# The second wq slice loaded through GpSimd's queue, x tiles 0 to 3 in order on SyncE's

## The chip, the cores and the metric

The kernel runs on one core of a Trainium2 chip. A core has five engines that run side by side, each with its own list of instructions: TensorE (PE in the profile; its weight loads are PEld), VectorE (DVE), ScalarE (ACT), GpSimd (POOL) and SyncE (SP), which here only issues transfers. SyncE, ScalarE and GpSimd each have a queue of their own for transfers; the transfers themselves run on the core's 16 DMA engines. Engines wait for one another through semaphores.

The metric is the time of one execution on the device in microseconds (us), the median of several runs.

## The reference

Two blocks work on the same x of 2048 tokens by 640 features (bfloat16), and a gate mixes them:

```
q, k, v = split(x @ wqkv)              # 32 heads of 20
phi(t)  = (t + 1 if t > 0 else exp(t)) + 1e-6
a = (phi(q) @ (phi(k)^T v)) / (phi(q) . sum(phi(k)) + 1e-6) @ wo      # per head
h = gelu(layernorm(x) @ w1), its four column quarters shifted by 1, -1, 2, -2 tokens, @ w2
x1 = x + h ;  b = x1 + gelu(layernorm(x1) @ w3) @ w4
out = g * a + (1 - g) * b,   g = sigmoid(x . gate_w)
```

Only the first lines matter here: the change lies in the first microseconds, in which the q of the first 512 tokens is made.

## The kernel before

Tokens are cut into 16 tiles of 128, features into five slices of 128 (KD = 5). The weights of q, wq, are five slices of 128 rows by 640 columns, one load of 160 KB each; an x tile is one load of the same size. A product of q for one tile needs x transposed, so for tiles 0 to 3 TensorE transposes the five 128 by 128 blocks of a tile into PSUM (`t_x`, matmuls of line 617) and VectorE copies them to `xT` (line 671). From tile 4 on the transposing is done by transfers (line 285).

`q_four` makes q for tiles 0 to 3. It hands to `stream` a list of steps, which TensorE runs in exactly this order: (t, None) is the transposing of tile t, (t, k) adds the product of tile t with slice k to the tile's accumulator, by one matmul of 512 columns (line 889) and one of 128 (line 890). When a tile has had its fifth slice, `phi` evacuates it: an exponential on ScalarE (line 662), a minimum and an addition (line 628) and the last combination (line 645) on VectorE. An accumulator takes two of the eight PSUM banks, and a bank is given out again when its evacuation is done. The list is written so that a step stands about where its tile or slice is expected.

Behind `q_four` come the k products of tile 0 (`k_first`, line 910) and then of tiles 1 to 3 (line 606), and from there on q and k tile by tile; then the sums over tokens on TensorE and VectorE, the two layernorm blocks and the output. All of these are items that a planner (`_Items.run`) strings together: it takes at each step the item that can start first by a model of costs (`_Sched.simulate`), which also gives out the PSUM banks. Within `q_four` nothing is planned.

The loads of the start are issued in program order on their queues. Before the change ScalarE's queue has slice 0 of wq, and SyncE's has x tiles 0, 1 and 3, slice 1, x tile 2, slices 2, 3 and 4, the five slices of wk, the gate weights, and x tiles 4 to 7 in one load (lines 690 to 699, through the helpers at lines 679 to 686; the issuing instruction is always line 289, the gate weights' line 288). GpSimd begins with a memset of two columns of wkg (line 688), and then makes constants (lines 725 to 739): the identity for the transposes, masks, zeros. Its own queue is used later, for w1, w2, wv and wo.

Of the kernel before, what the change touches and what calls it, by code (L numbers as in the profile page):

```python
# [416 lines left out]
def _build(nc, A_x, A_wqkv, A_wo, B_w1, B_w2, B_w3, B_w4, gate_w, out, dbg=None, stop=None):  # L417
# [246 lines left out]
    def memset(engf, ap, val):  # L664
        return engf(lambda e: e.memset(ap, val), [], [ap])
# [19 lines left out]
    def load_wq(k, queue="sp"):  # L685
        sch.dma(queue, wq[:, k, :], A_wqkv[128 * k:128 * (k + 1), 0:D], "wq%d" % k)

    memset(pool, wkg[:, :, D:D + 2], 1.0)
    load_wq(0, "act")
    for load, i in ((load_x, 0), (load_x, 1), (load_x, 3), (load_wq, 1), (load_x, 2), (load_wq, 2), (load_wq, 3), (load_wq, 4)):  # L690
        load(i)
    for k in range(KD):
        dma_in(wkg[:, k, 0:D], A_wqkv[128 * k:128 * (k + 1), D:2 * D], "wk%d" % k)
# [67 lines left out]
    def phi(b, dst, after_exp=None):  # L761
        n = nfree(dst)
        er = Er[:, slot("E", 3), 0:n]
        src = psf[:, 512 * b:512 * b + n]
        activation(er, src, ACTF.Exp)
        if after_exp is not None:
            after_exp()
        ts(dve, er, er, 1.0, EPS_PHI, ALU.min, ALU.add)
        return stt(dst, src, 1.0 + EPS_PHI, er, ALU.add, ALU.max)
# [103 lines left out]
    def stream(order, w, n2, done):  # L873
        bs = {}
        for t, k in order:
            if k is None:
                if t is None:
                    warmup(WARM2, 0.42)
                else:
                    t_x(t)  # L880
                continue
            if k == 0:
                bs[t] = pair()
                bank_hold.update((bs[t], bs[t] + 1))
            b = bs[t]
            l = xT[:, k, 128 * t:128 * (t + 1)]

            def fn(e, l=l, b=b, k=k):
                e.matmul(ps[:, b, 0:512], l, w[:, k, 0:512], start=(k == 0), stop=(k == KD - 1))  # L889
                return e.matmul(ps[:, b + 1, 0:n2], l, w[:, k, 512:512 + n2], start=(k == 0), stop=(k == KD - 1))  # L890
            pe(fn, [w[:, k, 0:512 + n2], l], [ps[:, b, 0:512], ps[:, b + 1, 0:n2]], cost=272.0)
            if k == KD - 1:
                bank_hold.difference_update((b, b + 1))
                done(t, b)

    def q_four():
        order = [(1, None), (0, 0), (3, None), (1, 0), (0, 1), (1, 1), (3, 0), (3, 1), (2, None), (0, 2), (1, 2), (0, 3), (0, 4), (1, 3),
                 (1, 4), (3, 2), (3, 3), (3, 4), (2, 0), (2, 1), (2, 2), (2, 3), (2, 4)]
        stream(order, wq, 128, lambda t, b: phi(b, pq_tok[:, t + 1, :]))

    def k_out(t, b):
# [16 lines left out]
    addA(("tx", 0), 0.28, lambda: t_x(0, (0, 1, KD)))  # L918
    addA(("warm", 1), 0.0, lambda: warmup(WARM2, 0.42))
    addA(("q", 3), 5.44, q_four)  # L920
    addA(("k", 0), 1.36, k_first)
    for i in range(1, 4):
# [399 lines left out]
    for t in range(NT):  # L1322
        deps = [(("zb",), 1.0), (("qr", max(t // 4, 1)), 2.0)]
        if t < 7:
            i = (5 * t) // 2 + 3
# [3 lines left out]
        else:  # L1329
            i = 3 * (t - 7)  # L1330
# [41 lines left out]
    order = IT.run(sch, hook)  # L1372
# [6 lines left out]
def bass_gated_mix__linear_attn_block__mixer_s_mlp__prompt_kernel(  # L1379
    nc, A_x, A_wqkv, A_wo, B_x, B_w1, B_w2, B_w3, B_w4, gate_w, out  # L1380
):
    assert tuple(A_x.shape) == (1, S, D) and tuple(out.shape) == (1, S, D)
    assert tuple(A_wqkv.shape) == (D, 3 * D) and tuple(A_wo.shape) == (D, D)
    assert tuple(B_w1.shape) == (D, D) and tuple(B_w2.shape) == (D, D)
    assert tuple(B_w3.shape) == (D, F) and tuple(B_w4.shape) == (F, D) and tuple(gate_w.shape) == (D,)
    _build(nc, A_x, A_wqkv, A_wo, B_w1, B_w2, B_w3, B_w4, gate_w, out)
# [28 lines left out]
```

## Time and profile before

| what | value |
|---|---|
| median of three runs | 260.2 us (259.57 to 260.27) |
| profiled execution | 260.19 us |
| its span (first to last instruction) | 258.4 us |
| TensorE busy | 252.7 us, 98% of the span |
| granted TensorE clock | 1.0 |
| VectorE, ScalarE, GpSimd busy | 158.5, 110.9, 97.0 us |

The span is shorter than the execution, since launching and finishing lie around it. Times in the profile are counted from the start of the span. A busy TensorE need not be TensorE at its peak. A transfer has two times: that of its issue, which holds the issuing engine, and that of its landing, for which others wait. "Idle before" is the time for which an engine stood still ahead of an instruction, with what ended it. A wait for several semaphores is put down to the one that came last.

The order on SyncE's queue before, by start in us: x tile 0 at 0.79, x tile 1 at 1.25, x tile 3 at 1.71, slice 1 of wq at 2.18, x tile 2 at 2.66, slices 2 to 4 from 3.13, the wk slices from 4.55, the gate weights at 6.93, x tiles 4 to 7 at 7.40.

### The profile page before, as it was taken

The page shows a single profiled execution, that of the slowest core. Times are in us where ns is not written, and L with a number is a line of the kernel's source. Part 1 is how long each engine was busy: PE and PEld are TensorE (multiplying, and loading weights), DVE is VectorE, ACT ScalarE, POOL GpSimd, SP SyncE. Part 2 cuts the span into 40 slices and gives each one's busy share as a digit, 9 for nine tenths or more (in the row PEclk, how much of TensorE's full clock was granted, in tenths as well). Part 3 has the DMA queues.
Part 4 walks back from the last instruction along what each step waited for, and adds up shares of the span by engine and source line. Part 5 has one row for each costly group of instructions (what it writes and reads, how often), then busy time and mean ns, then how long its engine had stood idle before and what let it go on. Part 6 is the DMA issues. An engine that isn't in the chain of part 4 may idle for free.

```text
span 258.4 us, 3797 instructions
## 1 busy us (share of the span) xinstructions
PE 252.7 (98%) x1400; PEld 122.0 (47%) x1427; DVE 158.5 (61%) x293; ACT 110.9 (43%) x229; POOL 97.0 (38%) x154
## 2 busy tenths in 40 slices
PE   7999999999999999999999999999999999999996
PEld 2555555544445455555444444444444444444443
DVE  2597877899954699989995302999022530134076
ACT  1496777741355856694864240005500045200100
POOL 8004996869944119659681210111020120021000
PEclk9999999999999999999999999999999999999999
DMA  6858997826528699483667512114200140000324
GB/s 193 264 94 239 140 138 196 231 56 122 102 46 108 115 382 322 85 100 65 127 123 118 101 20 23 25 25 129 43 3 0 20 124 0 0 0 1 43 84 139
DMA packets 58644, 26.78 MB, mean 104 GB/s; under 512 B 49966, under 2 KB 57215, under 8 KB 58626
## 3 DMA queue, kind: packets, MB, share of 16 engines
q1 hardware_dynamic: 57122, 22.92, 42.6%
q0 software_dynamic: 1168, 3.28, 5.5%
q10 hardware_dynamic: 336, 0.35, 0.4%
q8 instruction: 11, 0.18, 0.3%
q14 instruction: 7, 0.06, 0.1%
HBM read 12.09 MB, written 2.67 MB: 57 GB/s over the span
## 4 chain that ended last, share of the span: by engine, by line
PE 80%; DVE 12%; DMA 3%; ACT 2%; issue 1%; SPq 1%; DVEq 0%
PE ps L606 53%; PE ps L1229 22%; DVE qprod L636 7%; DMA wq<-in_A_wqkv_dram 2%; DVE x_tok L643 2%; PE ps L889 1%; ACT h2T L662 1%; PE ps L788 1%; DMA xnT<-xn 1%; PE ps L1116 1%; DVE pq_tok L1143 1%; PE ps L1204 1%; DVE dnr L1126 1%; ACT junk L661 1%; DVE zsum L636 1%
## 5 line engine op out<-in xcount | busy, mean ns | idle before, releaser
L606 PE MATMUL ps<-xnT,w 128*128 128x512 bf16 x351 | 80.0, 379 | 0.6 <-DMA xnT<-xn 0.2
L606 PEld LDWEIGHTS ps<-xnT,w 128*128 128x128 bf16 x360 | 34.6, 98 | 39.3
L645 DVE SCALAR_TENSOR_TENSOR x_tok<-ps,stg,abx 128x512 bf16<-128x512 f32 (+2 forms) x17 | 12.2, 717 | 58.2 <-PE ps L1229 48.4
L1229 PE MATMUL ps<-w,h2T 128*128 128x512 bf16 (+2 forms) x215 | 46.4, 366 | 0.3
L628 POOL TENSOR_SCALAR abx<-x_tok,stg 128x512 f32<-128x512 bf16 x16 | 12.1, 756 | 88.1 <-DVE x_tok L645 70.0
L628 POOL TENSOR_SCALAR xn<-x_tok,st 128x640 bf16<-128x640 bf16 x32 | 38.6, 1219 | 8.8 <-DMA xnT<-xn 8.4
L662 ACT ACTIVATE h2T<-ps 128x512 bf16<-128x512 f32 x52 | 29.8, 599 | 22.8 <-PE ps L606 22.8
L1229 PEld LDWEIGHTS ps<-w,h2T 128*128 128x128 bf16 x221 | 21.1, 98 | 24.1
L662 ACT ACTIVATE tlT<-ps 128x512 bf16<-128x512 f32 x8 | 4.8, 597 | 64.1 <-PE ps L606 41.9
L662 ACT ACTIVATE Er<-ps 128x640 bf16<-128x640 f32 (+1 forms) x35 | 23.0, 659 | 17.8 <-PE ps L606 9.6
L661 ACT ACTIVATE junk<-x_tok 128x640 bf16<-128x640 bf16 x32 | 23.6, 737 | 4.7 <-DVE x_tok L643 4.2
L662 ACT ACTIVATE hsT<-ps 128x512 bf16<-128x512 f32 (+1 forms) x32 | 18.9, 594 | 14.2 <-PE ps L606 13.8
L606 PE MATMUL ps<-w,hsT 128*128 128x128 bf16 (+1 forms) x159 | 23.8, 298 | 0.1
L606 PE MATMUL ps<-wkg,xT 128*128 128x512 bf16 (+1 forms) x148 | 22.5, 298 | 0.2
L606 PE MATMUL ps<-M_sb,pqnT 128*128 128x512 bf16 x78 | 19.3, 379 | 0.2
L606 PEld LDWEIGHTS ps<-w,hsT 128*128 128x128 bf16 x160 | 13.4, 98 | 12.5
L645 DVE SCALAR_TENSOR_TENSOR abx<-ps,stg,abx 128x512 f32<-128x512 f32 x16 | 12.0, 749 | 10.7 <-PE ps L606 7.2
L606 PEld LDWEIGHTS ps<-wkg,xT 128*128 128x128 bf16 x150 | 12.6, 97 | 11.7
L808 PE MATMUL ps<-pk_tok,x_tok 128*128 128x512 bf16 x78 | 17.7, 379 | 0.1
L643 DVE SCALAR_TENSOR_TENSOR x_tok<-ps,x_tok 128x640 bf16<-128x640 f32 x16 | 13.1, 821 | 7.5 <-PE ps L606 6.9
L636 DVE TENSOR_TENSOR qprod<-qprod,pk_tok 128x640 f32<-128x640 f32 x13 | 16.3, 1253 | 0.5
L628 DVE TENSOR_SCALAR Er<-Er 128x640 bf16<-128x640 bf16 (+1 forms) x35 | 11.6, 332 | 7.6 <-ACT Er L662 6.8
(85 smaller groups left out, 280.7 us busy)
## 6 DMA issues: line engine op xcount, KB each, us to landing
w<-in_B_w_dram SPq DMA_DIRECT2D x1, 2160.0 KB, 9.7
w<-in_B_w_dram SPq DMA_DIRECT2D x1, 2080.0 KB, 15.4
x_tok<-in_A_x_dram SPq DMA_DIRECT2D x3, 640.0 KB, 5.7
out_dram<-x_tok SPq DMA_DIRECT2D x3, 640.0 KB, 3.5
w<-in_B_w_dram POOLq DMA_DIRECT2D x8, 160.0 KB, 5.9
wkg<-in_A_wqkv_dram SPq DMA_DIRECT2D x5, 160.0 KB, 4.1
wv<-in_A_wqkv_dram POOLq DMA_DIRECT2D x1, 800.0 KB, 5.7
x_tok<-in_A_x_dram SPq DMA_DIRECT2D x4, 160.0 KB, 3.3
```

Source lines behind the costliest of these rows:

```text
L606: ins = e.matmul(out_ap, l, r, start=(i == 0), stop=(i == n - 1))
L628: return engf(lambda e: e.tensor_scalar(out_ap, in_ap, s1, s2, op0, op1), rd, [out_ap], cost=cost)
L636: return engf(lambda e: e.tensor_tensor(out_ap, a, b_, op), [a, b_], [out_ap], cost=cost)
L643: return dve(lambda e: e.scalar_tensor_tensor(out_ap, in0, scalar, in1, op0, op1, accum_out=accum), rd, [out_ap, accum], cost=cost + 70.0)
L645: return dve(lambda e: e.scalar_tensor_tensor(out_ap, in0, scalar, in1, op0, op1), rd, [out_ap], cost=cost)
L661: return act(lambda e: e.activation(out_ap, in_ap, func, bias=bias, scale=scale, accum_out=accum), rd, wr, cost=cost)
L662: return act(lambda e: e.activation(out_ap, in_ap, func, bias=bias, scale=scale), rd, wr, cost=cost)
L788: e.matmul(ps[:, b, :], l, x_tok[:, t, 0:512], start=(t == 0), stop=(t == NT - 1))
L808: ins = e.matmul(ps[:, b, :], l, r, start=(t0 + q_ == 0), stop=(t0 + q_ == NT - 1))
L889: e.matmul(ps[:, b, 0:512], l, w[:, k, 0:512], start=(k == 0), stop=(k == KD - 1))
L1116: ins = e.matmul(o, l, r, start=st, stop=sp)
L1229: ins = e.matmul(o, l, r, start=False, stop=(i == KFF - 1), skip_group_check=shared)
```

## The change

Slice 1 of wq is loaded through GpSimd's queue, by the second of GpSimd's instructions, between the memset of wkg and the constants. SyncE's queue loses this load and has x tiles 0 to 3 in order, then slices 2, 3 and 4. TensorE's list in `q_four` has tiles 2 and 3 exchanged, and the step (2, 2) stands ahead of (0, 3).

```
@@ -686,8 +686,9 @@
         sch.dma(queue, wq[:, k, :], A_wqkv[128 * k:128 * (k + 1), 0:D], "wq%d" % k)
 
     memset(pool, wkg[:, :, D:D + 2], 1.0)
+    load_wq(1, "pool")
     load_wq(0, "act")
-    for load, i in ((load_x, 0), (load_x, 1), (load_x, 3), (load_wq, 1), (load_x, 2), (load_wq, 2), (load_wq, 3), (load_wq, 4)):
+    for load, i in ((load_x, 0), (load_x, 1), (load_x, 2), (load_x, 3), (load_wq, 2), (load_wq, 3), (load_wq, 4)):
         load(i)
     for k in range(KD):
         dma_in(wkg[:, k, 0:D], A_wqkv[128 * k:128 * (k + 1), D:2 * D], "wk%d" % k)
@@ -894,8 +895,8 @@
                 done(t, b)
 
     def q_four():
-        order = [(1, None), (0, 0), (3, None), (1, 0), (0, 1), (1, 1), (3, 0), (3, 1), (2, None), (0, 2), (1, 2), (0, 3), (0, 4), (1, 3),
-                 (1, 4), (3, 2), (3, 3), (3, 4), (2, 0), (2, 1), (2, 2), (2, 3), (2, 4)]
+        order = [(1, None), (0, 0), (2, None), (1, 0), (0, 1), (1, 1), (2, 0), (2, 1), (3, None), (0, 2), (1, 2), (2, 2), (0, 3), (0, 4),
+                 (1, 3), (1, 4), (2, 3), (2, 4), (3, 0), (3, 1), (3, 2), (3, 3), (3, 4)]
         stream(order, wq, 128, lambda t, b: phi(b, pq_tok[:, t + 1, :]))
```

More of the change, by code (lines that the diff above doesn't have):

```diff
@@ L688, in _build @@
     memset(pool, wkg[:, :, D:D + 2], 1.0)
+    load_wq(1, "pool")
     load_wq(0, "act")
-    for load, i in ((load_x, 0), (load_x, 1), (load_x, 3), (load_wq, 1), (load_x, 2), (load_wq, 2), (load_wq, 3), (load_wq, 4)):
+    for load, i in ((load_x, 0), (load_x, 1), (load_x, 2), (load_x, 3), (load_wq, 2), (load_wq, 3), (load_wq, 4)):
         load(i)
@@ L896, in q_four @@
     def q_four():
-        order = [(1, None), (0, 0), (3, None), (1, 0), (0, 1), (1, 1), (3, 0), (3, 1), (2, None), (0, 2), (1, 2), (0, 3), (0, 4), (1, 3),
-                 (1, 4), (3, 2), (3, 3), (3, 4), (2, 0), (2, 1), (2, 2), (2, 3), (2, 4)]
+        order = [(1, None), (0, 0), (2, None), (1, 0), (0, 1), (1, 1), (2, 0), (2, 1), (3, None), (0, 2), (1, 2), (2, 2), (0, 3), (0, 4),
+                 (1, 3), (1, 4), (2, 3), (2, 4), (3, 0), (3, 1), (3, 2), (3, 3), (3, 4)]
         stream(order, wq, 128, lambda t, b: phi(b, pq_tok[:, t + 1, :]))
```

## The prediction

> **What bounds the kernel now.** I read the page first (busy time, the chain that ended last), then the chain in order of time, then the timeline of the first 13 us, and last the transfers.
>
> ```profile
> span 258.4 us, 3797 instructions
> PE 252.7 (98%) x1400; PEld 122.0 (47%) x1427; DVE 158.5 (61%) x293; ACT 110.9 (43%) x229; POOL 97.0 (38%) x154
> PE 80%; DVE 12%; DMA 3%; ACT 2%; issue 1%; SPq 1%; DVEq 0%
> ...
> 2.18 4.37 DMA wq<-in_A_wqkv_dram
> 6.55 0.05 issue
> 6.60 0.39 PE ps L889
> ```
>
> TensorE is busy for 252.7 of 258.4 us, so a change at the start can win only what TensorE idles there, and what it wins or loses is handed on whole. The chain names the first link: it runs back from the first product with the second wq slice (6.60) to that slice's load, issued at 2.18 on SyncE's queue and landed at 6.55. Nothing in front of that load is late but its place in the queue. The timeline shows what TensorE does meanwhile (start, duration, engine, line, and in brackets the idle time before with what ended it):
>
> ```profile
> 3.80 0.28 PEld L617 LDWEIGHTS ps<-ident,x_tok 128*128 128x128 bf16 x5 [1.16 <-DMA x_tok<-in_A_x_dram]
> 4.34 0.45 PE L617 MATMUL ps<-ident,x_tok 128*128 128x128 bf16 x5
> 4.63 0.38 PE L889 MATMUL ps<-wq,xT 128*128 128x512 bf16 x1
> 5.36 0.45 PE L617 MATMUL ps<-ident,x_tok 128*128 128x128 bf16 x5 [0.29 <-DMA x_tok<-in_A_x_dram]
> 5.64 0.38 PE L889 MATMUL ps<-wq,xT 128*128 128x512 bf16 x1
> 6.60 0.39 PE L889 MATMUL ps<-wq,xT 128*128 128x512 bf16 x1 [0.52 <-DMA wq<-in_A_wqkv_dram]
> ...
> 6.88 0.38 PE L889 MATMUL ps<-wq,xT 128*128 128x512 bf16 x1
> 7.70 0.44 PE L617 MATMUL ps<-ident,x_tok 128*128 128x128 bf16 x5
> 7.97 0.38 PE L889 MATMUL ps<-wq,xT 128*128 128x512 bf16 x1
> 11.78 1.53 PE L910 MATMUL ps<-wkg,xT 128*128 128x512 bf16 x10
> ```
>
> These are, in order: transposes of x tile 0 (3.80), of tile 1 (4.34), product (tile 0, slice 0) at 4.63, transposes of tile 3 (5.36, after a wait for its load), product (1, 0) at 5.64, product (0, 1) at 6.60 after the wait for slice 1, and so on to the first product with slice 2 at 7.97. A product (a wide and a narrow matmul) is issued every 6.88 - 6.60 = 0.28 us, 0.27 by the chain's finer pieces, and five transposes take the same. So without the wait (0, 1) would start at 5.64 + 0.27 = 5.91: the wait for slice 1 costs 0.69 us, and the one for tile 3 costs 5.36 - 4.90 = 0.46 ahead of it. From 6.60 to the start of the k products at 11.78 the order runs without a gap.
>
> **The change part by part.** One 160 KB load (163.8 kB) leaves SyncE's queue and goes to GpSimd's, right behind the small memset of wkg. Tile 2 takes tile 3's place, third on SyncE's queue; tile 3 is fourth; slices 2 to 4 and everything behind them (five wk slices, the gate weights, x tiles 4 to 7) move one place up. TensorE's order is the old one with 2 and 3 exchanged, and product (2, 2) drawn ahead of (0, 3). It is still 20 products and four sets of transposes, so no work is added on TensorE, VectorE or ScalarE.
>
> (a) GpSimd's own time.
>
> ```profile
> 0.79 0.11 POOL L665 MEMSET wkg<- 128x10 bf16 x1 [0.29 <-POOLq L1400]
> 1.11 0.29 POOL L674 TENSOR_SCALAR_AFFINE_SELECT ident<-ones_c 128x128 bf16<-128x128 bf16 x1
> 18.32 0.26 POOL L628 TENSOR_SCALAR st<-lr 128x4 f32<-128x4 f32 x1 [11.21 <-ACT lr L662]
> L289 POOL DMA_DIRECT2D w<-in_B_w_dram x8: 513/562/656, 35.7 to 39.6; - x8
> ...
> L289 POOL DMA_DIRECT2D w<-in_B_w_dram x5: 872/893/1112, 25.4 to 29.1; - x5
> ```
>
> A load of this very form (128 rows of 1280 bytes, half of the eight w2 loads) holds GpSimd 0.51 to 0.66 us, and the first of the dearer w1 loads 1.11. The identity for the transposes is then done at 1.40 + 0.66 = 2.1, at worst 2.5, and the first transpose waits for x until 3.80: cost nothing, with 1.3 us to spare. The other constants follow; GpSimd then idles 11.21 us before 18.32, which swallows the rest. Without that cover each would cost its 0.66 us.
>
> (b) When slice 1 lands. The trace of before has no load on GpSimd's queue at the start, so the price is bounded by its later loads, from issue to landing, min/median/max. The first row is of the first five w1 loads (256 and 64 byte runs, the first of them into an idle queue), the second of the eight w2 loads, the third of all sixteen.
>
> ```profile
> DMA to landing us min/median/max: 3.4/6.4/7.2
> DMA to landing us min/median/max: 5.0/5.6/6.0
> DMA to landing us min/median/max: 3.4/5.9/8.8
> ```
>
> Issued at 0.79 + 0.11 = 0.90, it lands between 4.3 and 9.7. I take the lower end, since the queue is empty and only the first w1 load had that; the eight w2 loads stood in one line behind others. I add one load's own time on shared engines, 0.44 (below): 4.7. It is wanted at 5.91 or later.
> The Trainium skill, "DMA: Bandwidth & Descriptors" (Anatomy of one DMA — SWDGE path), prices a GpSimd load at 2.0 us plus bytes over 436 GB/s; by it, my estimate is a landing at about 0.90 + 0.66 + 2.4 = 4.0. No row here shows so short a one.
>
> (c) What the earlier load pushes back. Bytes moved, in half-microsecond windows (after the clock, the DMA engines' busy share and GB/s):
>
> ```profile
> 1.50:2.00 0.50, 0.50 (x2) 0.15 (x1) 0.00 (x0) 0.50 (x1) 0.41 (x2) 1.00 0.41 46
> 2.00:2.50 0.50, 0.50 (x3) 0.15 (x2) 0.00 (x0) 0.50 (x1) 0.39 (x2) 1.00 0.66 92
> 2.50:3.00 0.50, 0.50 (x3) 0.14 (x1) 0.00 (x0) 0.04 (x1) 0.42 (x3) 1.00 0.90 328
> 3.00:3.50 0.50, 0.50 (x2) 0.00 (x0) 0.00 (x0) 0.00 (x0) 0.50 (x1) 1.00 1.08 389
> 3.50:4.00 0.50, 0.24 (x5) 0.20 (x5) 0.00 (x0) 0.00 (x0) 0.50 (x5) 1.00 1.06 366
> 4.00:4.50 0.50, 0.47 (x9) 0.30 (x7) 0.43 (x2) 0.00 (x0) 0.50 (x1) 1.00 0.96 154
> 4.50:5.00 0.50, 0.50 (x7) 0.23 (x5) 0.39 (x2) 0.00 (x0) 0.50 (x1) 1.00 0.59 141
> 5.00:5.50 0.50, 0.21 (x5) 0.15 (x4) 0.33 (x1) 0.00 (x0) 0.50 (x1) 1.00 0.91 297
> ```
>
> From 2.5 to 4.0 the engines are full (366 to 389 GB/s), so 163.8 kB put in there push what stands behind them by 163.8 / 370 = 0.44 us. Tile 1's transposes, at 4.34 the first thing that this can delay for good, move to 4.78 and (0, 0) to 5.07. Tile 2 is now the fifth load by bytes where tile 3 was the fourth. The rows also show a dip from 4.0 to 5.0 (141 to 154 GB/s) whose cause they don't tell, and tile 2 has to come through it. Early bound: no dip. 611 kB are moved by 4.00, five loads are 819, the other 208 at 370 GB/s last to 4.56; tile 1, third, had its 492 kB at 3.67 and its transposes at 4.34, so 0.67 later: 5.23. Late bound: the fifth load of before, slice 1 itself: 6.60. I take what is nearest, the third load of the same queue with one load more ahead of it: 5.36 + 0.44 = 5.80. Then (1, 0) comes at 5.80 + 0.28 = 6.08 and (0, 1) at 6.35 in place of 6.60: a gain of 0.25.
>
> (d) The slices behind. Issue (start, duration for three) and landing of the wq loads of before:
>
> ```profile
> 3.13 1.38 SPq L289 DMA_DIRECT2D wq<-in_A_wqkv_dram  x3
> ...
> DMA to landing us min/median/max: 3.2/4.2/4.4
> ```
>
> Slice 2 landed by 3.13 + 4.4 = 7.53 at the latest, as the seventh load, and it is the seventh again. It is wanted 7.97 - 6.60 = 1.37 after (0, 1), at 7.72: no wait. Slices 3 and 4 follow 0.46 and 0.92 later (by 8.0 and 8.45) and are wanted three products later (8.54) and at 8.81: covered. If slice 2 is not there, 0.2 us of the gain go. The wk slices and x tiles 4 to 7 leave earlier and are wanted 0.25 earlier: nothing.
>
> (e) The reordered products. The evacuation of tile 0 starts one product (0.27) later against TensorE; the first k product takes over tile 0's accumulators.
>
> ```profile
> 10.36 0.82 DVE L645 SCALAR_TENSOR_TENSOR pq_tok<-ps,Er 128x640 bf16<-128x640 f32 x1
> ```
>
> It was done at 11.18, 0.60 ahead of 11.78; 0.33 is left: nothing. Past 11.78 all follows TensorE, or the additions on VectorE that start when the k products end, and shifts as one.
>
> **The sum.** The profiled execution took 260.19 us, 1.8 around its span of 258.4, and the three runs' median is 260.2. 260.19 - 0.25 = 259.94, 259.9.
>
> **The rivals.**
> A, the forecast: tile 2 through the dip, 259.9.
> B, the dip goes with the load that left (it lies where slice 1's packets were due) or no longer falls on TensorE's inputs. Tile 2 is there at 5.23, TensorE is ready for it at 5.07 + 0.27 = 5.34, so (0, 1) comes at 5.34 + 0.56 = 5.90: gain 0.70, 259.5. If tile 1 isn't pushed either, the copy of its transposes bounds it, which ends at 4.07 + 1.26 = 5.33:
>
> ```profile
> 4.07 1.26 DVE L671 COPY xT<-ps 128x128 bf16<-128x128 bf16 x3 [4.07 <-PE ps L617]
> ```
>
> (1, 0) at 5.37, (0, 1) at 5.64: gain 0.96, 259.2. For it: engines at 59% busy in the dip. Against: a queue that hands on less than it could may do so again.
> C, only the wait's name changes: bytes decide, tile 2 as the fifth load is as late as the fifth was, its transposes start at 6.60, (0, 1) at 6.60 + 0.55 = 7.15: 0.55 slower, 260.7. It decides from a landing past 6.05. For it: the same five loads stand ahead. Against: the fifth load's own slow packets would have to wander to x. The Trainium skill, "DMA: Bandwidth & Descriptors" (Issuing engines are not separate DMA queues), speaks for C: all queues end on the same 16 engines, another queue saves only the issue. The full windows agree, the half-idle dip doesn't.
> D, slice 1 comes late through GpSimd. At 5.6 us from issue it lands at 6.5 and leaves next to no gain; past 5.65 it is a loss; at 8.8 it lands at 9.7 and (0, 1) comes at 9.75, 3.15 later: 263.3. For it: the w2 rows, the same form. Against: the idle queue.
> E, the planner that interleaves everything behind the first tiles goes by estimated times, and its estimate of the start changes; another order may result, for good or ill.
>
> ```profile
> 52.45 0.57 issue
> ```
>
> A wait of the size of this one, gained or lost once or twice, is 0.6 to 1.2 us.
>
> **How the numbers follow.** A 0.32, B 0.29, C 0.13, D 0.16, E 0.10. A measurement of this kernel tells about 0.3% from no change, 0.78 us. Faster by more: half of B (its upper half passes 0.78) and half of E, 0.20. Slower by more: two thirds of D, a third of C (tile 2 later still), half of E, 0.20. The rest, 0.60, is within. The range goes from B's end, 259.2, to 261.0, which leaves out most of D and part of E; A's own is 259.6 to 260.2.
>
> **What would show it.** (b) slice 1 landed before 5.9, no wait for wq left at line 889; (c) tile 1's transposes near 4.8 and a wait for x in front of tile 2's, near 5.8; (d) the first product with slice 2 near 7.7 and without a wait; (e) the k products at 11.5; afterwards the same instructions in the same order, all 0.25 earlier. The prediction is wrong where the wait for wq stays, where the first transposes of tile 0 wait longer than to 4.2, or where the two traces part after 12 us.

## The result and the profile after

The changed kernel took 260.64 us (median of 22 runs, 260.16 to 262.75), the kernel before beside it 260.12 (22 runs, 259.57 to 260.27): a ratio of 1.0038, 95% interval 1.0022 to 1.0053. It is slower, by 0.4%, where 0.1% faster was forecast. The median hides something: the times fall into two groups. Fifteen runs lie between 260.16 and 260.85 (median 260.53, 0.41 over the kernel before) and seven between 261.88 and 262.75 (median 262.11, another 1.6). Of all runs of the kernel before, in every comparison below, the longest is 260.77.

The execution that was profiled is one of the seven: 261.96 us, 1.77 over the 260.19 of the profiled one before. The page of the changed kernel (span and busy times):

```profile
span 260.2 us, 3797 instructions
...
PE 254.8 (98%) x1400; PEld 123.5 (47%) x1427; DVE 158.4 (61%) x293; ACT 110.8 (43%) x229; POOL 97.9 (38%) x155
```

TensorE is busy 2.1 us longer with the same number of instructions, so it did not wait longer, it worked more slowly. After the start its order of instructions is the old one, and so are those of VectorE and ScalarE. The chain in order of time names the new first link, the load of tile 2 instead of the load of slice 1:

```profile
1.71 4.42 DMA x_tok<-in_A_x_dram
6.13 0.05 issue
6.18 0.71 PE ps L617 x5
```

The timeline of the changed kernel (lines 889, 890 and 910 of before are 890, 891 and 911 here):

```profile
1.35 0.77 POOL L289 DMA_DIRECT2D wq<-in_A_wqkv_dram  x1 [0.46 <-issue]
2.43 0.29 POOL L674 TENSOR_SCALAR_AFFINE_SELECT ident<-ones_c 128x128 bf16<-128x128 bf16 x1
3.75 0.71 PE L617 MATMUL ps<-ident,x_tok 128*128 128x128 bf16 x5 [0.21 <-DMA x_tok<-in_A_x_dram]
4.37 0.74 PE L617 MATMUL ps<-ident,x_tok 128*128 128x128 bf16 x5
4.90 0.63 PE L890 MATMUL ps<-wq,xT 128*128 128x512 bf16 x1
6.18 0.71 PE L617 MATMUL ps<-ident,x_tok 128*128 128x128 bf16 x5 [0.54 <-DMA x_tok<-in_A_x_dram]
6.68 0.63 PE L890 MATMUL ps<-wq,xT 128*128 128x512 bf16 x1
7.22 0.63 PE L890 MATMUL ps<-wq,xT 128*128 128x512 bf16 x1
9.69 0.10 PEld L890 LDWEIGHTS ps<-wq,xT 128*128 128x128 bf16 x1
9.74 0.38 PE L890 MATMUL ps<-wq,xT 128*128 128x512 bf16 x1
13.55 1.52 PE L911 MATMUL ps<-wkg,xT 128*128 128x512 bf16 x10
```

Two things are to be seen. First, no product waits for wq any more, but tile 2's transposes wait for x until 6.18, where tile 3's stood at 5.36. Second, a product of 512 columns takes 0.63 us until about 9.5 and 0.38 from then on; before, the one at 4.63 already took 0.38, and the first transposes ran at the short duration too, 0.45 in place of 0.71. Products are issued every 0.54 us (7.22 - 6.68) instead of 0.27: half rate. In both kernels TensorE begins with six matmuls of constants (`warmup`), at half rate: six of 512 columns in 2.72 us. The rows of before:

```profile
0.83 2.72 PE L857 MATMUL ps<-const-bfloat16-1.0 128*128 128x512 bf16 x6 [0.83 <-PEq L1400]
3.81 0.45 PE L617 MATMUL ps<-ident,x_tok 128*128 128x128 bf16 x5 [0.26 <-DMA x_tok<-in_A_x_dram]
```

The 1.77 us follow from these rows. At the full rate (0, 1) would have come at 6.18 + 0.55 = 6.73, 0.13 later than the 6.60 of before. It came at 7.22, 0.49 later still, at half rate. From there to the first product with slice 2 it is 9.74 - 7.22 = 2.52 in place of 1.37, another 1.15. 0.13 + 0.49 + 1.15 = 1.77, and the k products start that much later: 13.55 in place of 11.78. All behind shifts as one.

The half-microsecond windows (the last three numbers are the granted clock, the DMA engines' share and GB/s) and the landings of the changed kernel, slices 0 and 1 in the first row of landings, x tiles 1 to 3 in the second:

```profile
3.50:4.00 0.50, 0.29 (x4) 0.25 (x4) 0.00 (x0) 0.00 (x0) 0.36 (x2) 1.00 1.10 294
4.00:4.50 0.50, 0.50 (x8) 0.50 (x6) 0.23 (x1) 0.00 (x0) 0.49 (x2) 1.00 0.71 259
4.50:5.00 0.50, 0.50 (x7) 0.50 (x6) 0.42 (x1) 0.00 (x0) 0.50 (x2) 1.00 1.12 228
5.00:5.50 0.50, 0.50 (x4) 0.05 (x1) 0.35 (x1) 0.00 (x0) 0.50 (x4) 1.00 0.74 218
```

```profile
DMA to landing us min/median/max: 3.1/3.8/4.4
```

```profile
DMA to landing us min/median/max: 3.0/4.4/4.4
```

The column of the granted clock reads 1.00 while the matmuls take double, but there it says nothing: the trace's record of the clock begins only at 9.57 us, with the full clock, and this view counts a stretch without a record as 1.00. In the kernel before the record begins at 3.70. So it is the durations that show the rate here. The dip is shallower but lasts longer, to 5.5. Slice 1 was issued at 1.35 and landed 4.4 us later, at 5.80; tile 1 landed as early as before and tile 2 at 6.13.

### The profile page after: what moved, and what is told of

Its sections match the earlier page's. It is cut to its first block, busy times and chain, and to the rows that moved or that the text cites. A ratio compares the mean times of both kernels' runs of the same rounds, so it can differ in the third digit from the quotient of the medians.

```text
span 260.2 us, 3797 instructions
## 1 busy us (share of the span) xinstructions
PE 254.8 (98%) x1400; PEld 123.5 (47%) x1427; DVE 158.4 (61%) x293; ACT 110.8 (43%) x229; POOL 97.9 (38%) x155
## 4 chain that ended last, share of the span: by engine, by line
PE 79%; DVE 12%; DMA 3%; ACT 3%; issue 1%; SPq 1%; DVEq 0%
PE ps L606 51%; PE ps L1230 22%; DVE qprod L636 7%; PE ps L890 2%; DMA x_tok<-in_A_x_dram 2%; DVE x_tok L643 2%; ACT h2T L662 1%; DMA xnT<-xn 1%; PE ps L789 1%; PE ps L1117 1%; ACT junk L661 1%; DVE pq_tok L1144 1%; PE ps L1205 1%; DVE dnr L1127 1%; PE ps L891 1%
```

## The experiments

The theory from this profile has two parts: the load through GpSimd's queue delays the third load of SyncE's queue by more than its bytes, and the long wait that results keeps TensorE at half rate. The rivals are that bytes alone or the exchange of tiles 2 and 3 make the delay, and that the half rate comes and goes without the wait. In some of these kernels something is added that the result doesn't need: idle matmuls (the two filled kernels), or a "spare" load into memory that is not yet in use. Ratios are to the kernel before, unless said otherwise. The "upper group" is the runs past 261.8 (in e1_filled all six are, for a reason of their own); six other runs of these kernels lie between the two groups, at 261.08 to 261.56, and stay unexplained.

### The wait filled

The changed kernel with two matmuls of constants in TensorE's list ahead of tile 2's transposes. First they took an accumulator bank like any other work; then they were written to a bank without that bookkeeping.

```
-        order = [(1, None), (0, 0), (2, None), (1, 0), (0, 1), (1, 1), (2, 0), (2, 1), (3, None), (0, 2), (1, 2), (2, 2), (0, 3), (0, 4),
+        order = [(1, None), (0, 0), (None, None), (2, None), (1, 0), (0, 1), (1, 1), (2, 0), (2, 1), (3, None), (0, 2), (1, 2), (2, 2), (0, 3), (0, 4),
...
-                    warmup(WARM2, 0.42)
+                    warmup(1024, 0.42)
```

> The changed kernel with two idle matmuls of 512 columns put in TensorE's list where it waits for x tile 2, and nothing else. Theory G (half rate): in part of the runs TensorE stays at half rate until past 9 us, because the wait for tile 2 leaves it too idle; with the wait filled no run is past 261.2 us, the median is 260.2 to 260.5, and no 512-column matmul of line 890 takes 0.63 us after 7 us. Rival L (late load only): the spread is that of the load; the median stays at 260.6 and about a third of the runs are past 261.8.

Measured: 263.81 (6 runs), 1.0134 [1.0107, 1.0162], far slower. The fill did bring the full rate from about 6.7, but taking a bank moved tile 3's accumulator onto banks that were still in use, and its first product waited for the second evacuation, which by the order of the list is tile 1's (done at 13.08). Then TensorE fell back to half rate:

```profile
13.14 0.39 PE L890 MATMUL ps<-wq,xT 128*128 128x512 bf16 x1 [2.02 <-DVE pq_tok L645]
13.86 0.63 PE L890 MATMUL ps<-wq,xT 128*128 128x512 bf16 x1
```

This fall the clock column does show:

```profile
13.50:14.00 0.50, 0.50 (x5) 0.27 (x3) 0.50 (x1) 0.00 (x0) 0.00 (x0) 0.52 0.00 0
16.50:17.00 0.50, 0.50 (x3) 0.15 (x1) 0.47 (x2) 0.00 (x0) 0.00 (x0) 0.57 0.21 43
```

By the trace's record the clock was full from 6.69, at 0.50 from 13.52 to 16.93, and full from there on. So this run tells of the fill only what happens before 10.9. It was made again without the banks:

```
-                    warmup(WARM2, 0.42)
+                    sch.op("pe", lambda e: [e.matmul(ps[:, 0, :], one(128), one(512), start=True, stop=True) for _ in range(2)][-1], cost=0.0)
```

> The changed kernel with two idle matmuls of 512 columns in TensorE's list where it waits for x tile 2, now into a bank that is free anyway and without a place in the giving out of banks, so that the accumulators stay where the changed kernel has them (in the first filled kernel tile 3's accumulator fell on tile 0's and waited 2 us). Theory G (half rate kept by the long wait): no run past 261.2 us, median 260.1 to 260.5, full rate at the latest from about 7 us. Rival L (late load only): median 260.6 and a quarter to a third of the runs past 261.8, as the changed kernel.

Measured: 260.72 (11 runs, 260.5 to 261.21), 1.0024 [1.0015, 1.0033]. No run lies in the upper group, and the full rate is there before the wait for tile 2 ends:

```profile
4.98 0.53 PE L890 MATMUL ps<-wq,xT 128*128 128x512 bf16 x1
5.40 0.60 PE L879 MATMUL ps<-const-bfloat16-1.0 128*128 128x512 bf16 x2
6.26 0.45 PE L617 MATMUL ps<-ident,x_tok 128*128 128x128 bf16 x5 [0.26 <-DMA x_tok<-in_A_x_dram]
6.55 0.38 PE L890 MATMUL ps<-wq,xT 128*128 128x512 bf16 x1
```

The upper group goes with the wait. The lower one stays, and the median is higher than expected. In the profiled run the late tile costs 0.21 (the k products start at 11.99 in place of 11.78); its span is 0.4 longer than before, and the rest of that arises only after 20 us and isn't explained.

### The wait without GpSimd, and the names alone

The kernel before with tile 3 behind slice 1 on SyncE's queue, so that its transposes wait longer and the wait for wq goes:

```
-    for load, i in ((load_x, 0), (load_x, 1), (load_x, 3), (load_wq, 1), (load_x, 2), (load_wq, 2), (load_wq, 3), (load_wq, 4)):
+    for load, i in ((load_x, 0), (load_x, 1), (load_wq, 1), (load_x, 3), (load_x, 2), (load_wq, 2), (load_wq, 3), (load_wq, 4)):
```

> The kernel before with slice 1 ahead of x tile 3 on SyncE's queue, so that TensorE has one long wait (for tile 3, the fifth load) instead of two short ones, and nothing goes through GpSimd. Theory G: tile 3 comes at 6.1 to 6.6, median 260.4 to 260.9, and part of the runs are past 261.8 with TensorE at half rate past 7 us. If the half rate belongs to GpSimd's load: median 260.6 at most and no run past 261.2.

Measured: 260.15 (12 runs), 1.0006 [0.9989, 1.0023]: the median is not the 260.4 to 260.9 of theory G. But two of the twelve stand at 262.17 and 262.18, one of them the profiled one, and that group is theory G's. It has the half rate until about 10.2, with nothing on GpSimd's queue:

```profile
5.95 0.71 PE L617 MATMUL ps<-ident,x_tok 128*128 128x128 bf16 x5 [0.29 <-DMA x_tok<-in_A_x_dram]
9.66 0.63 PE L889 MATMUL ps<-wq,xT 128*128 128x512 bf16 x1
10.50 0.38 PE L889 MATMUL ps<-wq,xT 128*128 128x512 bf16 x1
```

The upper group needs no load through GpSimd; one late x tile is enough.

The kernel before with the names of tiles 2 and 3 exchanged, in the loads and in the list of products:

```
-    for load, i in ((load_x, 0), (load_x, 1), (load_x, 3), (load_wq, 1), (load_x, 2), (load_wq, 2), (load_wq, 3), (load_wq, 4)):
+    for load, i in ((load_x, 0), (load_x, 1), (load_x, 2), (load_wq, 1), (load_x, 3), (load_wq, 2), (load_wq, 3), (load_wq, 4)):
...
-        order = [(1, None), (0, 0), (3, None), (1, 0), (0, 1), (1, 1), (3, 0), (3, 1), (2, None), (0, 2), (1, 2), (0, 3), (0, 4), (1, 3),
+        order = [(1, None), (0, 0), (2, None), (1, 0), (0, 1), (1, 1), (2, 0), (2, 1), (3, None), (0, 2), (1, 2), (0, 3), (0, 4), (1, 3),
```

> The kernel before with x tiles 2 and 3 exchanged in the loads and in the products, and nothing else. All theories: 260.1, as before, within 0.1%, and no run past 260.6.

Measured: 260.02 (12 runs), 0.9999 [0.9989, 1.0009]. The exchange costs nothing.

### The same load on ScalarE's queue

The changed kernel with slice 1 as the second load of ScalarE's queue, run on two occasions:

```
-    load_wq(1, "pool")
     load_wq(0, "act")
+    load_wq(1, "act")
```

> The changed kernel with slice 1 as the second load on ScalarE's queue instead of GpSimd's. If the bytes ahead of tile 2 decide, whatever the queue: tile 2 still lands near 6.1, the transposes of tile 2 start at 6.0 to 6.3, median 260.4 to 260.8. If GpSimd's queue is what makes it late (it starts late, its packets are larger): tile 2 lands by 5.6, median 259.9 to 260.2.

> The kernel with slice 1 as ScalarE's second load once more, for its interval and a second profile. If it beats the kernel before: ratio 0.998 to 0.9995 with the interval below 1; tile 2 lands by 5.6 and no run is past 260.6. If the first measurement was luck: 1.000.

Measured: 259.76 (12 runs, 259.4 to 260.27), 0.9986 [0.9976, 0.9997], and 259.51 (11 runs, 259.4 to 260.1), 0.9986 [0.9977, 0.9995]. It beats both kernels, the one before by 0.14%, less than the 0.3% that this kernel's measurement is held to tell from no change, though neither interval reaches 1. Timeline and windows of the second:

```profile
5.29 0.45 PE L617 MATMUL ps<-ident,x_tok 128*128 128x128 bf16 x5
5.90 0.38 PE L890 MATMUL ps<-wq,xT 128*128 128x512 bf16 x1
7.27 0.38 PE L890 MATMUL ps<-wq,xT 128*128 128x512 bf16 x1
```

```profile
4.00:4.50 0.50, 0.36 (x6) 0.19 (x4) 0.38 (x2) 0.00 (x0) 0.50 (x1) 1.00 1.09 394
4.50:5.00 0.50, 0.42 (x6) 0.39 (x7) 0.27 (x1) 0.00 (x0) 0.50 (x1) 1.00 1.00 318
```

The dip is gone, tile 2's transposes start at 5.29 without a marked wait, and (0, 1) comes at 5.90: rival B of the prediction to the hundredth, only through another queue than the change used.

Then the same with (0, 1) drawn ahead of tile 2's transposes:

```
-        order = [(1, None), (0, 0), (2, None), (1, 0), (0, 1), (1, 1), (2, 0), (2, 1), (3, None), (0, 2), (1, 2), (2, 2), (0, 3), (0, 4),
+        order = [(1, None), (0, 0), (0, 1), (2, None), (1, 0), (1, 1), (2, 0), (2, 1), (3, None), (0, 2), (1, 2), (2, 2), (0, 3), (0, 4),
```

> The kernel with slice 1 as ScalarE's second load, and product (0, 1) drawn ahead of the transposes of tile 2, where TensorE waited for tile 2 and for the copy of tile 1. If those two waits (about 0.4 us in that profile) are filled by it: first product with slice 2 at 7.0 to 7.1 in place of 7.27, median 259.4 to 259.6. If the waits only move behind tile 2: 259.76 as without it.

Measured: 260.1 (11 runs), 1.0 [0.9987, 1.0014]. No better than the plain version, and not clearly worse, since the intervals overlap; one run took 261.45. (0, 2) came at 7.46, not near 7.0. Tile 2 landed at 5.54 this time (5.25 in e12_act_again, with the same loads), and the wait only moved behind it.

And the changed kernel with tile 2 on ScalarE's queue and slice 1 back on SyncE's:

```
-    load_wq(1, "pool")
     load_wq(0, "act")
-    for load, i in ((load_x, 0), (load_x, 1), (load_x, 2), (load_x, 3), (load_wq, 2), (load_wq, 3), (load_wq, 4)):
+    load_x(2, "act")
+    for load, i in ((load_x, 0), (load_x, 1), (load_wq, 1), (load_x, 3), (load_wq, 2), (load_wq, 3), (load_wq, 4)):
```

> The changed kernel with x tile 2 as ScalarE's second load, and slice 1 third on SyncE's queue: again five loads ahead of (0, 1), on two queues of the same kind, but the slice on the queue where it was. If the dip in the bytes moved at 4 to 5 us (141 to 154 GB/s before) comes when SyncE's queue is alone, it is gone here too: over 330 GB/s in 4.0 to 5.0, median 259.7 to 260.0. If it comes with slice 1 on SyncE's queue: under 250 GB/s there, slice 1 lands past 5.4, median 260.0 to 260.4.

Measured: 259.79 (10 runs), 0.9989 [0.998, 0.9998], and the dip is mostly closed:

```profile
4.00:4.50 0.50, 0.50 (x6) 0.39 (x4) 0.23 (x1) 0.00 (x0) 0.50 (x1) 1.00 1.06 384
4.50:5.00 0.50, 0.50 (x6) 0.38 (x5) 0.42 (x1) 0.00 (x0) 0.50 (x1) 1.00 0.98 269
```

For the dip it matters little which load goes to ScalarE's queue, as long as a second one does.

### The changed kernel again, and its load as the first instruction

The changed kernel unedited, and with GpSimd's load ahead of the memset of wkg.

```
+    load_wq(1, "pool")
     memset(pool, wkg[:, :, D:D + 2], 1.0)
-    load_wq(1, "pool")
```

> The changed kernel once more, for its spread and a second profile. Theory G: two groups, near 260.5 and past 261.8, a sixth to a half of the runs in the second; a profile from the first group has full rate by 7 us and the same late landings (tile 2 near 6.1), one from the second has half rate past 9 us. Theory L: where a run is slow, tile 2 is late by as much.

Measured: 261.14 (8 runs), 1.0049 [1.0024, 1.0074], three of eight in the upper group. In the profiled run, one of the three, tile 2 is later still:

```profile
7.02 0.72 PE L617 MATMUL ps<-ident,x_tok 128*128 128x128 bf16 x5 [1.32 <-DMA x_tok<-in_A_x_dram]
7.53 0.63 PE L890 MATMUL ps<-wq,xT 128*128 128x512 bf16 x1
9.66 0.44 PE L890 MATMUL ps<-wq,xT 128*128 128x512 bf16 x1
```

> The changed kernel with GpSimd's load as its first instruction, ahead of the memset. If the load is late because it starts late (1.35 us in the changed kernel, not 0.90): it starts near 0.8, slice 1 and tile 2 land 0.4 to 0.5 earlier (tile 2 by 5.7), median 260.0 to 260.4, fewer runs past 261.8. If the start doesn't matter: tile 2 past 6.1, median 260.5 to 261.2.

Measured: 260.83 (8 runs), 1.0049 [1.0026, 1.0072], three of eight in the upper group. The load did not start earlier, so whether its late start matters was not tried by this. The profiled run is of the lower group, and gives the price of the late tile at full rate:

```profile
1.32 0.77 POOL L289 DMA_DIRECT2D wq<-in_A_wqkv_dram  x1 [0.82 <-POOLq L1401]
6.29 0.45 PE L617 MATMUL ps<-ident,x_tok 128*128 128x128 bf16 x5 [0.68 <-DMA x_tok<-in_A_x_dram]
6.85 0.38 PE L890 MATMUL ps<-wq,xT 128*128 128x512 bf16 x1
```

(0, 1) at 6.85 is 0.25 behind the 6.60 of before, and this execution took 260.42: 0.23 more than the 260.19.

### The queue's effect by itself

The kernel before, untouched in all that it needs, with a spare load of 160 KB added, first on GpSimd's queue, then as the second load on ScalarE's:

```
+    sch.dma("pool", w3[:, 0, 0:D], A_wqkv[128:256, 0:D], "spare")
     load_wq(0, "act")
```

```
     load_wq(0, "act")
+    sch.dma("act", w3[:, 0, 0:D], A_wqkv[128:256, 0:D], "spare")
```

> The kernel before with one load added that nobody needs: slice 1's rows once more, through GpSimd's queue behind the memset, into a buffer that is filled much later. It measures what such a load does to the others. Theory Q (GpSimd's queue costs the others more than its bytes): tile 3's transposes start at 6.0 or later (5.36 before), median 260.6 to 261.2. Theory bytes: 163.8 kB at 370 GB/s, tile 3 at 5.7 to 5.9, median 260.3 to 260.6, the same as the spare load on ScalarE's queue.

> The kernel before with the same spare load as ScalarE's second. Theory Q: tile 3's transposes start by 5.7, no dip below 250 GB/s between 4.0 and 5.0, median 259.9 to 260.3. Theory bytes: tile 3 at 5.7 to 5.9, median 260.3 to 260.6, as on GpSimd's queue.

Measured: on GpSimd's queue 260.43 (10 runs), 1.003 [1.0008, 1.0051], three of ten in the upper group; on ScalarE's 259.98 (10 runs), 0.9999 [0.999, 1.0008], none there. Timeline and windows, GpSimd's first: tile 3's transposes, and the dip.

```profile
6.12 0.71 PE L617 MATMUL ps<-ident,x_tok 128*128 128x128 bf16 x5 [0.42 <-DMA x_tok<-in_A_x_dram]
```

```profile
4.00:4.50 0.50, 0.50 (x7) 0.50 (x6) 0.23 (x1) 0.00 (x0) 0.49 (x2) 1.00 0.90 254
4.50:5.00 0.50, 0.50 (x8) 0.50 (x6) 0.42 (x1) 0.00 (x0) 0.50 (x2) 1.00 0.85 223
```

```profile
5.25 0.45 PE L617 MATMUL ps<-ident,x_tok 128*128 128x128 bf16 x5
```

```profile
4.00:4.50 0.50, 0.26 (x5) 0.08 (x2) 0.48 (x2) 0.00 (x0) 0.50 (x1) 1.00 1.07 389
4.50:5.00 0.50, 0.47 (x6) 0.39 (x7) 0.17 (x1) 0.00 (x0) 0.50 (x1) 1.00 1.03 318
```

The same bytes, added to the same kernel, put tile 3's transposes at 6.12 through the one queue and at 5.25 through the other, where the kernel before has 5.36. Bytes don't make the delay; the queue does. The times are less clear: tile 3 came as theory Q said, but the median with GpSimd's spare, 260.43, lies in the range that the theory of bytes gave.

The landings show more than the transposes. With GpSimd's spare only the one load behind it is late: tile 3 landed at 6.07 (5.31 before), but slice 1 at 6.49 (6.55), tile 2 at 6.89 (6.96) and slice 2 at 7.33 (7.40). With ScalarE's spare the same loads landed at 5.20, 6.06, 6.52 and 6.96, though 160 KB more were moved. And in all eight profiles with a load on GpSimd's queue the third load of SyncE's queue landed 0.28 to 0.43 behind that load, whenever it came: from 5.55 and 5.93 with both spares (below) to 6.69 and 6.98 in e8_again.

The Trainium skill, "DMA: Bandwidth & Descriptors" (Issuing engines are not separate DMA queues), says that transfers run on the same 16 engines whichever engine issued them and that another queue saves only the issue. These two runs differ from it by 0.87 us for one load.

Then both spares, and a quarter of the spare (32 rows, 40 KB) on GpSimd's queue:

```
+    sch.dma("pool", w3[:, 0, 0:D], A_wqkv[128:256, 0:D], "spare0")
     load_wq(0, "act")
+    sch.dma("act", w3[:, 1, 0:D], A_wqkv[128:256, 0:D], "spare1")
```

```
+    sch.dma("pool", w3[0:32, 0, 0:D], A_wqkv[128:160, 0:D], "spare0")
     load_wq(0, "act")
```

> The kernel before with two spare loads of 160 KB, one as ScalarE's second and one as GpSimd's first. Theory R (a load through GpSimd's queue delays the others by itself): tile 3's transposes, at 5.25 with ScalarE's spare load alone, start at 6.0 or later, and the dip between 4.0 and 5.5 is back; median 260.5 or more. Theory S (GpSimd's load only fails to close the dip that ScalarE's longer queue closes, and costs its bytes): tile 3 at 5.6 to 5.8, over 330 GB/s from 4.0 to 5.0; median 260.0 to 260.3.

> The kernel before with a spare load of 40 KB (32 rows) through GpSimd's queue in place of the 160 KB. If the delay goes with GpSimd's bytes: a quarter of 0.76, tile 3's transposes at 5.5 to 5.6 (5.36 before, 6.12 with 160 KB), median 260.0 to 260.2, no run past 261.8. If any load through GpSimd's queue delays the others: tile 3 at 5.9 or later, median 260.3 or more, some runs past 261.8.

Measured: both, 260.31 (10 runs), 1.0012 [1.0, 1.0024], none in the upper group; a quarter, 260.28 (10 runs), 1.0015 [0.9999, 1.0032], one of ten at 262.03. Neither time is clear of the kernel before, and one run with both spares, 261.56, lies between the groups. Tile 3's transposes with both spares:

```profile
5.97 0.45 PE L617 MATMUL ps<-ident,x_tok 128*128 128x128 bf16 x5 [0.18 <-DMA x_tok<-in_A_x_dram]
```

and with the quarter:

```profile
6.08 0.45 PE L617 MATMUL ps<-ident,x_tok 128*128 128x128 bf16 x5 [1.10 <-DMA x_tok<-in_A_x_dram]
```

With both, GpSimd's 163.8 kB cost 5.97 - 5.25 = 0.72 over ScalarE's spare alone, where bytes at 370 GB/s would cost 0.44; the dip was closed (448 and 307 GB/s from 4.0 to 5.0), so the delay isn't only the dip. Neither theory came as stated: the tile was as late as theory R says, the time nearly that of theory S. A quarter of the bytes delayed as much as the whole: 6.08 beside 6.12, in one profile of each. So the delay belongs to the presence of a load on GpSimd's queue rather than to its size. By what mechanism it comes about, and what the dip is, no run here shows.

## Why the prediction was wrong, step by step

The 260.64 lies in the forecast range of 259.2 to 261.0, but on the other side of the kernel before: a gain of 0.25 was forecast, and a loss of 0.5 came. That the range holds it is luck: it was stretched for rivals whose reasons did not come.

(a) GpSimd's own time: right in that it costs nothing. The load held GpSimd 0.77 us (forecast 0.51 to 0.66, at worst 1.11), and the identity was done at 2.43 + 0.29 = 2.72, later than the 2.5 called the worst, since the load started late, but a whole microsecond ahead of its use at 3.75.

(b) Slice 1: right in what it concluded, wrong in the number. No product waits for wq. But the load was issued at 1.35, not at 0.90, and took 4.4 us instead of 3.8, so it landed at 5.80 and not at 4.7. Had tile 2 been on time, it would have been close: rival B needed it at 5.90. The Trainium skill, "DMA: Bandwidth & Descriptors" (Anatomy of one DMA — SWDGE path), whose formula gave an estimate of 4.0, is further off than the nearest row of the trace.

(c) What the earlier load pushes back: this is the step that failed. It took the delay from bytes at the full engines' rate (0.44) and added it to 5.36, for 5.80. (The rate was also read a little high: from 2.5 to 3.0 its row has 328 GB/s, not 366 to 389.) Measured: 6.18 in the profiled run, so the term of 0.44 is 0.82, which alone turns the gain of 0.25 into a loss of 0.13 (6.73 against 6.60). It was 6.26, 6.29, 6.52 and 7.02 in the four other profiles with slice 1 on GpSimd's queue. The first thing that bytes should have pushed, tile 1's transposes, was not pushed at all: 4.37 beside 4.34. The spare loads show what stands in the step's place: a load on GpSimd's queue holds the one x tile behind it back by some 0.7 us, hardly depending on its size (transposes at 5.97 to 6.12 with it, at 5.25 to 5.53 without), and one on ScalarE's queue doesn't. The tile lands some 0.3 behind GpSimd's load, so the late slice of (b) and the late tile of (c) go together; the prediction took them for two things. Rival C (the wait only changes its name, decided by a landing past 6.05) is what happened at 6.13, though not for its reason, which was bytes. That its 260.7 stands beside the measured 260.64 is chance: it had the transposes at 6.60 and all products at full rate.

(d) The slices behind: right. The first product with slice 2 has no wait, at 9.74 in the profiled run and in its place 1.37 behind (0, 1) in the run of the same loads on ScalarE's queue (7.27 - 5.90).

(e) The reordered products cost nothing: right. The k products follow the last q product without a wait. The exchange of tiles alone measured 0.9999. Rival E did not come: the order of TensorE, VectorE and ScalarE after the start is unchanged.

What no step contained: TensorE's rate. Every term of the sum took a product at 0.27 us and five transposes at the same. In the profiles of this study the start of the full rate differs from run to run: at 3.5 to 3.7 in five kernels (the one before among them), between 4.1 and 5.6 in six others, at 6.7 in e1_filled, and between 9.5 and 10.3 in the four late profiles (the changed kernel twice, the spare on GpSimd's queue, and e3_x_later); none lies between 6.7 and 9.5. The Trainium skill, "TensorE: Matmul & The Clock Gate" (Part 1: The HAM clock gate), says that the array starts at half rate and is released after a busy window of some 3.4 us that runs freely, without regard to the start of the kernel. The traces agree with the step: in e1_filled the clock was at 0.50 for 16.93 - 13.52 = 3.41 us, and full for twice that before (6.69 to 13.52).

Counted back by one step of 3.41, the four late starts (9.57, 9.71, 9.78 and about 10.26) give 6.16, 6.30, 6.37 and 6.85. In these runs, then, a step ended at the end of the wait for the x tile or shortly behind it, and did not bring the full rate. In the eleven early ones it came by 5.6, ahead of that wait; in e9_pool_first, for one, it came near 5.4, and the wait of 0.68 behind it did no harm. By these traces it is chance, where the steps fall, that puts a run into one group or the other. The nearest reading is that a long idle time in a step spoils it. But idle time alone is not the rule: in the kernel before the step that ended at 3.70 held 0.69 us without a matmul (0.29 to 0.83 and 3.55 to 3.70) and released, in e3_x_later the one that ended at 6.85 held 0.52 (0.23 and 0.29) and didn't. What such a step counts stays open.

That the wait has part in it is shown from two sides. Filling it removes the upper group (0 of 11 in e5_filled_same_banks, against 10 of 30 for the changed kernel, 3 of 8 in e9_pool_first and 3 of 10 in e10_spare_pool), and in e1_filled, whose fill is the same up to there, a step that ended at 6.69, among those four ends, did release. And e3_x_later makes the group without that load (2 of 12). From what size on a wait does it isn't shown. Why the kernel before never shows it, with 0.46 and 0.52 us of idle time in the same place, is argued only. At half rate its products would take 0.53 each, and the two gaps would nearly fill by themselves: from transposes at 4.37, (0, 0) at 4.90, tile 3 at 5.43 (its load is there at 5.36), (1, 0) at 5.96 and (0, 1) ready at 6.5 against 6.60. Only 0.1 us would be idle, where the changed kernel idles 0.54 and e3_x_later 0.29 at half rate.

So of the 0.52 us of the median 0.41 stand in the lower group alone, 0.25 of them the late tile at full rate by e9_pool_first, the rest not taken apart. The upper group lifts the median by only 0.11, but a run that falls into it by 1.6, and about a third of the runs do.

## What to carry to other kernels

Here an early load that stood in another's way did better on ScalarE's queue than on GpSimd's, if by little (0.14% under the kernel before). Find out what a queue costs by a spare load added to the kernel as it is. In the first ten microseconds read the durations of TensorE's matmuls as well as its waits: merging two short waits into one long one can cost several times the wait, in a share of the runs that one profile doesn't show. Work that fills a gap must not go through whatever gives out buffers, or it moves everybody else's.

## What was not expected of the hardware

- The granted clock in the profile's rows stood at 1.00 while matmuls of 512 columns took 0.63 us in place of 0.38 and weight loads 0.15 in place of 0.10. The trace's record of the clock begins with its first change (at 9.57 in the changed kernel, 9.71 in e10_spare_pool, 3.70 before), and in seven of the sixteen traces there is none; what isn't recorded is counted as 1.00, in the mean clock of a run too.
- TensorE also falls back: after the wait of 2.02 us in e1_filled the products took 0.63 again, with the recorded clock at 0.50. The three slowest of its six runs have a mean clock of 0.993, as this one, and so has the slowest run of the changed kernel, 262.75. The Trainium skill, "TensorE: Matmul & The Clock Gate" (Part 1: The HAM clock gate), puts the return to half rate after an idle window of about 3.4 us; a shorter wait did it here.
- A load on GpSimd's queue started at 1.32 to 1.36 whether it stood in front of the memset or behind it, and landed 4.2 to 5.3 us later; the quarter of the size took 4.3.

- The 16 engines together dip to 123 to 179 GB/s from 4 to 5 us with one load on ScalarE's queue and the rest on SyncE's (the kernel before, e3_x_later and e4_names_only), and keep 318 to 394 with two loads on ScalarE's in e2_act_queue, e11_spare_act and e12_act_again. But in e6_act_early, with the loads of e12_act_again, they had 325 and then 238.
